# Local attention and two feed-forward layers in one kernel: the order of loads, attention units and weight decoding at the start

## The chip, the cores and the metric

The kernel runs on one core of one Trainium2 chip. The metric is the device time of one execution in microseconds (us). Before the change the median of 3 runs is 875.22 us (874.82 to 875.95).

## The reference

```python
def reference(**kwargs):
    attn_out = _attn_ref(...)                 # 4 batches, 8 heads, 512 local + 32 global rows, head size 64
    x = attn_out.transpose(0, 2, 1, 3).reshape(B * S, H * D)      # 2176 x 512
    x = _moe_ref(x=x, ...)                    # h = x @ w_in; g = elu(h); g @ w_out   (512 -> 2048 -> 512)
    return _moe2_ref(x=x, ...)                # rms norm; silu(xn @ w_gate) * (xn @ w_val) @ w_out
```

Local queries see the local keys within 32 positions and the 32 global keys; each row goes through a softmax. All weights arrive as 64-bit floats.

## The kernel before

**The pieces.** The attention of the local rows is cut into 16 units of 128 queries and all 8 heads (four units are one block of 512 rows). A unit has five pieces. `a_S` (L227) makes the scores: 8 mask matmuls with the `identr` matrix (L237) and 32 products of keys and queries from the tile `kq` (L243), into two tiles `s`. `a_E` (L247) takes the row maxima on the VectorE (DVE, L262 and L263) and the exponentials on the ScalarE (ACT, L265). `a_T` (L268) transposes the exponentials on the TensorE (PE, L271) and ACT copies them out (L273). `a_PV` (L276) multiplies them with the values of the tile `v` (L284). `a_N` (L288) divides by the row sums on DVE (L297 to L299) and writes the unit's part of `x`. When four units are done, `a_X` (L301) transposes the block on PE (L307), ACT rounds it to a high part (L308), and DVE takes what the rounding left, the low part (L309).

**The first expert layer.** `moe_block` (L339) then runs 16 steps over a block. Step j makes h with 12 matmuls (`mm1`, L132), the activation (ACT L121 and L122, DVE L123), its high and low part `g` (ACT L139, DVE L140), and one step later the second product with 12 matmuls (`mm2`, L153). The next block's attention units stand between these steps, a unit in every four of them.

**The weights.** `w_in` and `w_out` come as 16 raw tiles of 1 MB (512 x 512 doubles in two row groups), in the order of `order1`: two tiles of `w_in` and two of `w_out` for each group of four steps. A tile is decoded to a high and a low single-precision part in four operations: `w1_abs` on ACT (L85), `w1_bits` on DVE (L92, L93), `w1_hi` on ACT (L96), `w1_lo` on DVE (L99). Tiles 0 and 1 feed the first four steps of `mm1`, tiles 2 and 3 the first four of `mm2`. Raw tiles 0, 2, 4, ... share two buffers, so raw tile 4 may be loaded only after `w1_bits(0)`, and raw tile 6 only after `w1_bits(2)`.

**What sets the order.** All loads are issued by the SyncE (SP) in one queue. Eight of them can be under way: the ninth waits until the first has landed, and so on. PE runs in the order in which the program is written. In the stretch that the change touches, DVE and ACT do so too (`manual_schedule`, L419):

```python
        with tc.manual_schedule(engines={mybir.EngineType.DVE, mybir.EngineType.Activation}):
            nc.scalar.copy(identr, ident)
            ...
            w1_abs(0)
            a_S(0, ATT2)
            w1_bits(0)
            a_E(0)
            a_S(1, HB)
```

After that stretch, and for SP throughout, a scheduler that works when the kernel is built sets the order. Each engine executes in its order: an instruction that waits holds up all that stand behind it on that engine. The first four units take their keys and values in buffers of the weight pool (`load_kq` L208, `load_v` L217), so none of these loads waits for an earlier one to be used up. `a_X(0, (2, 3), ...)` puts its transposes into the two `h` buffers, so the first `mm1` must wait until DVE has read the third of the four.

**Later stages.** Block 0 decodes the tiles 3 to 15 between its steps; the blocks 1 and 2 prepare the second layer's weights; then come the global attention rows and the second expert layer, which begins after some 440 us and is bound by PE.

Of the kernel before, what the change touches and what calls it, by code (L numbers as in the profile page):

```python
# [40 lines left out]
def fused_kernel(ctx: ExitStack, tc: tile.TileContext, kq, vl, gkq, gv, w_in, w_out, w_gate, w_val, w_o2, rms_g, consts, out):  # L41
# [66 lines left out]
    def new_xT():  # L108
        return [moe.tile([P, 2, 512], F32R, tag=f"xT{c}", name=f"xT{c}") for c in range(4)]
# [84 lines left out]
    with ExitStack() as ls:  # L194
# [13 lines left out]
        def load_kq(u):  # L208
            if u < 16:
                if u < 4:  # L210
                    t = wpool.tile([P, 4, KC], F32, tag="w", name="kq0")
                else:
                    t = ap_.tile([P, 4, KC], F32, tag="kq", name="kq_")
                nc.sync.dma_start(out=t, in_=kq[u].rearrange("p (a n) -> p a n", a=4))
                kq_t[u] = t

        def load_v(u):  # L217
            if u < 16:
                if u < 4:
                    t = wpool.tile([P, 2112], F32, tag="w", name="v0")  # L220
                else:
                    t = ap_.tile([P, 2112], F32, tag="v", name="v_")
                t = t[:, :2080].rearrange("p (i h d) -> p i h d", i=4, h=8)
                nc.sync.dma_start(out=t, in_=vl[u].rearrange("p (i h d) -> p i h d", i=4, h=8))
                v_t[u] = t
# [50 lines left out]
        def a_PV(u, pools):  # L276
            e_t.pop(u)
            b, T = u // 4, u % 4
            ets, v = [et_t.pop((u, par)) for par in range(2)], v_t.pop(u)
            os_ = [pools[i][0].tile([P, 4, 65], F32, tag=pools[i][1], name="o") for i in range(2)]  # L280
            for par in range(2):
                for pr in range(4):
                    for i in range(4):
                        nc.tensor.matmul(os_[par][32 * i:32 * i + 32, pr, :], ets[par][:, pr * P + 32 * i:pr * P + 32 * i + 32], v[:, i, 2 * pr + par, :],  # L284
                                         start=True, stop=True)
            o_t[u] = os_
# [25 lines left out]
        ATT2 = [(aps, "att")] * 4  # L312
# [62 lines left out]
        def w1_load(n=1):  # L375
            for _ in range(n):
                i = n_raw[0]
                if i < 16:
                    wp = i % 2 == 1 and i < 12
                    raws[i] = dec_load(wpool if wp else dec["r"], "w" if wp else "raw", w_src(*order1[i]))  # L380
                    n_raw[0] += 1
# [3 lines left out]
        def w1_abs(i):  # L385
            dxs[i] = dec_abs(dec["t"], raws[i])

        def w1_bits(i):
            dec_bits(dxs[i], raws.pop(i))

        def w1_hi(i):
            kind, a, G = order1[i]
            dst = wpool.tile([P, 2, 2, 512], F32R, tag="w", name="wA")
            for k in range(2):
                if kind == "1":
                    W1[a + k, G] = dst[:, k]
                else:
                    W2[a + k] = dst[:, k]
            split_hi(dst, dxs[i])
            dsts[i] = dst  # L400

        def w1_lo(i):
            split_lo(dsts.pop(i), dxs.pop(i))
            n_dec[0] = i + 1
# [9 lines left out]

        HB = [(hps, "h")] * 2
        Y2 = [(yps, "y2"), (yps, "y3")]
        w1_load()
        load_v(0)
        with tc.manual_schedule(engines={mybir.EngineType.DVE, mybir.EngineType.Activation}):  # L419
            nc.scalar.copy(identr, ident)  # L420
            nc.scalar.copy(masks, mk)
            load_kq(1)
            load_v(1)
            w1_load()
            load_kq(2)
            load_v(2)
            load_kq(3)
            load_v(3)
            w1_load(3)
            w1_abs(0)  # L430
            a_S(0, ATT2)
            w1_bits(0)
            a_E(0)
            a_S(1, HB)
            a_T(0, 0, yps, "y0")
            a_T(0, 1, yps, "y1")
            w1_hi(0)
            a_E(1)
            a_PV(0, Y2)
            w1_lo(0)  # L440
            a_N(0)
            w1_abs(1)
            a_S(2, ATT2)
            a_T(1, 0, yps, "y0")
            a_T(1, 1, yps, "y1")
            a_E(2)
            w1_bits(1)
            a_PV(1, Y2)
            a_N(1)
            a_S(3, HB)  # L450
            a_T(2, 0, yps, "y0")
            a_T(2, 1, yps, "y1")
            a_E(3)
            w1_hi(1)
            a_PV(2, Y2)
            a_N(2)
            a_T(3, 0, yps, "y0")
            a_T(3, 1, yps, "y1")
            w1_lo(1)
            w1_abs(2)  # L460
            a_PV(3, Y2)
            a_N(3)
            xT_t = {0: new_xT()}
            a_X(0, (0, 1), xT_t[0], ATT2[:2] + HB)
            last = a_X(0, (2, 3), xT_t[0], ATT2[:2] + HB)
            w1_bits(2)
            w1_hi(2)
            w1_lo(2)
# [570 lines left out]
    for k in range(2):  # L1039
# [96 lines left out]
        for n in range(7):  # L1136
# [5 lines left out]
            last = n in (3, 5, 6)  # L1142
# [175 lines left out]
```

## Time and profile before

| | |
|---|---|
| median of 3 runs | 875.22 us |
| profiled execution, its own time | 874.71 us |
| its span, first to last instruction | 872.9 us |
| PE busy in matmuls | 847.9 us (97%) |
| DVE busy | 570.8 us (65%) |
| ACT busy | 461.8 us (53%) |
| moved by DMA | 165.69 MB, mean 190 GB/s |
| first `mm1` of block 0 begins | 39.65 us |

A profile shows one execution. "Busy" is the time in which an engine has an instruction at work. An instruction's row has its start, its length and, in brackets, how long the engine had been idle and which engine's work released it. "issue" as a releaser means that the profile shows nothing that the engine waited for. PEclk is the clock that TensorE was granted, as a share of its full 2.4 GHz; 0.5 is its lower level of 1.2 GHz. All times below count from the start of the span.

### The profile page before, as it was taken

The page shows a single profiled execution, that of the slowest core. Times are in us where ns is not written, and L with a number is a line of the kernel's source. Part 1 is how long each engine was busy: PE and PEld are TensorE (multiplying, and loading weights), DVE is VectorE, ACT ScalarE, POOL GpSimd, SP SyncE. Part 2 cuts the span into 40 slices and gives each one's busy share as a digit, 9 for nine tenths or more (in the row PEclk, how much of TensorE's full clock was granted, in tenths as well). Part 3 has the DMA queues.
Part 4 walks back from the last instruction along what each step waited for, and adds up shares of the span by engine and source line. Part 5 has one row for each costly group of instructions (what it writes and reads, how often), then busy time and mean ns, then how long its engine had stood idle before and what let it go on. Part 6 is the DMA issues. An engine that isn't in the chain of part 4 may idle for free.

```text
span 872.9 us, 16265 instructions
## 1 busy us (share of the span) xinstructions
PE 847.9 (97%) x6706; PEld 709.8 (81%) x6706; DVE 570.8 (65%) x1022; ACT 461.8 (53%) x790; POOL 8.0 (1%) x10
## 2 busy tenths in 40 slices
PE   4889999999999999999999999999999999999998
PEld 3667888888888888777878888878999888888998
DVE  3799737656575565544468787897987655555663
ACT  4688645555564455433264677764555444443442
POOL 0000000000000000000030000000000000000000
PEclk9899999999999999999999999999999999999999
DMA  9795625765687665442510687779623232329102
GB/s 361 314 376 191 258 84 188 263 240 200 222 280 285 220 230 210 168 165 97 161 36 25 213 294 242 251 249 330 264 73 120 73 97 74 97 65 404 62 25 86
DMA packets 92271, 165.69 MB, mean 190 GB/s; under 512 B 4900, under 2 KB 59428, under 8 KB 87076
## 3 DMA queue, kind: packets, MB, share of 16 engines
q1 hardware_dynamic: 92196, 164.65, 53.9%
q8 instruction: 53, 0.87, 0.4%
q14 instruction: 22, 0.18, 0.1%
HBM read 128.45 MB, written 36.18 MB: 189 GB/s over the span
## 4 chain that ended last, share of the span: by engine, by line
PE 90%; DMA 3%; ACT 3%; DVE 2%; issue 1%; POOL 0%; DVEq 0%; ACTq 0%
PE y L153 19%; PE h L132 19%; PE A L814 14%; PE c L1163 14%; PE Q L814 11%; DMA kq<-in_kq 2%; PE pg L828 2%; PE o L284 2%; PE s L243 2%; PE ptp L271 2%; PE yg L744 1%; PE og L848 1%; DMA ya<-yT 1%; PE go L966 1%; PE xtp L307 1%
## 5 line engine op out<-in xcount | busy, mean ns | idle before, releaser
L153 PE MATMUL y<-g,wA 128*128 128x512 f32 x768 | 195.8, 398 | 3.7 <-DVE g L140 2.5
L132 PE MATMUL h<-xT,wA 128*128 128x512 f32 x768 | 186.6, 392 | 1.3 <-DVE xT L309 1.3
L153 PEld LDWEIGHTS y<-g,wA 128*128 128x128 f32 x768 | 139.6, 188 | 38.4 <-issue 5.3
L132 PEld LDWEIGHTS h<-xT,wA 128*128 128x128 f32 x768 | 143.6, 188 | 32.1 <-DVE xT L309 1.5
L814 PE MATMUL A<-xc,wS 128*128 128x512 f32 x576 | 138.9, 392 | 0.1
L814 PEld LDWEIGHTS A<-xc,wS 128*128 128x128 f32 x576 | 107.0, 188 | 23.2 <-DVE pp L867 0.8
L1163 PE MATMUL c<-wH,p 128*128 128x256 f32 x1008 | 125.3, 283 | 0.0
L1163 PEld LDWEIGHTS c<-wH,p 128*128 128x128 f32 x1008 | 123.0, 192 | 0.2
L814 PE MATMUL Q<-xc,wS 128*128 128x512 f32 x432 | 104.4, 390 | 0.7 <-DVE t L858 0.7
L814 PEld LDWEIGHTS Q<-xc,wS 128*128 128x128 f32 x432 | 80.2, 188 | 17.5 <-DVE t L858 1.2
L858 DVE TENSOR_TENSOR t<-t,Q 128x512 f32<-128x512 f32 x72 | 48.9, 684 | 48.9 <-ACT t L861 33.7
L853 ACT CAST p<-pp 128x512 fp32r<-128x512 f32 x84 | 51.3, 620 | 55.7 <-PE c L1163 50.8
L121 ACT ACTIVATE e<-h 128x512 f32<-128x512 f32 x48 | 28.8, 600 | 95.9 <-PE h L132 95.9
L861 ACT COPY t<-A 128x512 f32<-128x512 f32 x72 | 42.0, 586 | 62.2 <-PE A L814 62.1
L854 DVE TENSOR_TENSOR p<-pp,p 128x512 fp32r<-128x512 f32 x84 | 56.7, 686 | 21.6 <-ACT p L853 21.6
L123 DVE SCALAR_TENSOR_TENSOR e<-e,h 128x512 f32<-128x512 f32 x48 | 32.8, 683 | 55.1 <-ACT e L122 54.8
L619 DVE TENSOR_TENSOR wS<-wraw,wS 128x1024 fp32r<-128x1024 f32 x42 | 51.2, 1218 | 15.2 <-ACT wS L618 15.1
L139 ACT CAST g<-e 128x512 fp32r<-128x512 f32 x64 | 39.8, 621 | 34.7 <-DVE e L123 21.3
L140 DVE TENSOR_TENSOR g<-e,g 128x512 fp32r<-128x512 f32 x64 | 44.0, 688 | 19.3 <-ACT g L139 18.8
L618 ACT CAST wS<-wraw 128x1024 fp32r<-128x1024 f32 x42 | 43.9, 1045 | 2.0 <-DMA wraw<-wS 2.0
L864 ACT ACTIVATE t<-t 128x512 f32<-128x512 f32 x36 | 22.8, 632 | 39.0 <-DVE t L858 39.0
L93 DVE SCALAR_TENSOR_TENSOR dx<-raw,dx 128x1024 int32<-128x1024 int32 x34 | 41.6, 1229 | 0.9
(201 smaller groups left out, 892.9 us busy)
## 6 DMA issues: line engine op xcount, KB each, us to landing
wH<-wH SPq DMA_DIRECT2D x20, 1024.0 KB, 8.7
wraw<-wS SPq DMA_DIRECT2D x36, 512.0 KB, 4.2
raw<-in_moe_w_out SPq DMA_DIRECT2D x14, 1024.0 KB, 6.6
raw<-in_moe_w_in SPq DMA_DIRECT2D x8, 1024.0 KB, 7.0
raw<-in_moe_w_gate SPq DMA_DIRECT2D x6, 1024.0 KB, 5.9
raw<-in_moe_w_val SPq DMA_DIRECT2D x6, 1024.0 KB, 5.8
wS<-raw SPq DMA_DIRECT2D x24, 256.0 KB, 2.3
gvr<-in_gv SPq DMA_DIRECT2D x8, 640.0 KB, 4.2
```

The source lines that it names most:

```text
L93: nc.vector.scalar_tensor_tensor(out=i32(x), in0=word[:, :, 0], scalar=29, in1=i32(x), op0=ALU.logical_shift_right, op1=ALU.bitwise_or)
L132: nc.tensor.matmul(h[:, :n], W1[c, G][:, ws, o:o + P], xT[c][:, xs, :n], start=(k == 0), stop=(k == 11))
L140: mark[:] = hi, nc.vector.tensor_tensor(out=g[:, 1, :n], in0=e[:, :n], in1=f(g[:, 0, :n]), op=ALU.subtract)
L153: nc.tensor.matmul(ys[dc][:, :n], W2[j][:, ws, dc * P:(dc + 1) * P], g[:, gs, :n], start=(j == 0 and k == 0), stop=(j == 15 and k == 2))
L618: nc.scalar.copy(t[:, :, 0, :], raw)
L619: nc.vector.tensor_tensor(out=t[:, :, 1, :], in0=raw, in1=f(t[:, :, 0, :]), op=ALU.subtract)
L814: nc.tensor.matmul(ps, w[:, 2 * (q % 4) + c, ws, :], x[:, c, xs, :], start=(first and c == 0 and z == 0), stop=(c == 1 and z == 2), skip_g ...
L853: hi = nc.scalar.copy(p[:, 0, :], src)
L854: mark[:] = hi, nc.vector.tensor_tensor(out=p[:, 1, :], in0=src, in1=f(p[:, 0, :]), op=ALU.subtract)
L858: mark[1] = nc.vector.tensor_tensor(out=t, in0=t, in1=ps, op=ALU.add)
L861: mark[0] = nc.scalar.copy(t, ps)
L1163: nc.tensor.matmul(ch[t // 2][:, 256 * (t % 2):256 * (t % 2) + 256], p[:, pl, t * P:(t + 1) * P], w[:, wl, :], start=(n in (0, 1, 3) and i ...
```

## The change

Before, the loads of raw weight tiles and of the units' keys and values alternate, and the decoding of tiles 0, 1 and the first operation of tile 2 is laid between the pieces of the units. The change issues the keys and values of the units 0 to 3 first (raw tile 0 ahead of the last values, raw tiles 1 to 3 behind them). It moves all decoding behind `a_PV(2)`: tile 0 goes between the last pieces of the units 2 and 3, tile 1 begins between the two halves of `a_X` and is finished after it, together with tile 2. On PE, `a_S(2)` moves ahead of `a_PV(0)`, and `a_S(3)` ahead of `a_PV(1)`. No instruction is added or dropped, and no size is changed.

```diff
--- before.py
+++ after.py
@@ -414,55 +414,54 @@
 
         HB = [(hps, "h")] * 2
         Y2 = [(yps, "y2"), (yps, "y3")]
+        load_kq(1)
+        load_v(0)
+        load_kq(2)
+        load_v(1)
+        load_kq(3)
+        load_v(2)
         w1_load()
-        load_v(0)
+        load_v(3)
+        w1_load(3)
         with tc.manual_schedule(engines={mybir.EngineType.DVE, mybir.EngineType.Activation}):
             nc.scalar.copy(identr, ident)
             nc.scalar.copy(masks, mk)
-            load_kq(1)
-            load_v(1)
-            w1_load()
-            load_kq(2)
-            load_v(2)
-            load_kq(3)
-            load_v(3)
-            w1_load(3)
-            w1_abs(0)
             a_S(0, ATT2)
-            w1_bits(0)
             a_E(0)
             a_S(1, HB)
             a_T(0, 0, yps, "y0")
             a_T(0, 1, yps, "y1")
-            w1_hi(0)
             a_E(1)
+            a_S(2, ATT2)
             a_PV(0, Y2)
-            w1_lo(0)
             a_N(0)
-            w1_abs(1)
-            a_S(2, ATT2)
             a_T(1, 0, yps, "y0")
             a_T(1, 1, yps, "y1")
             a_E(2)
-            w1_bits(1)
+            a_S(3, HB)
             a_PV(1, Y2)
             a_N(1)
-            a_S(3, HB)
             a_T(2, 0, yps, "y0")
             a_T(2, 1, yps, "y1")
             a_E(3)
-            w1_hi(1)
             a_PV(2, Y2)
+            w1_abs(0)
             a_N(2)
             a_T(3, 0, yps, "y0")
             a_T(3, 1, yps, "y1")
+            w1_bits(0)
+            a_PV(3, Y2)
+            w1_hi(0)
+            a_N(3)
+            xT_t = {0: new_xT()}
+            w1_lo(0)
+            a_X(0, (0, 1), xT_t[0], ATT2[:2] + HB)
+            w1_abs(1)
+            last = a_X(0, (2, 3), xT_t[0], ATT2[:2] + HB)
+            w1_bits(1)
+            w1_hi(1)
             w1_lo(1)
             w1_abs(2)
-            a_PV(3, Y2)
-            a_N(3)
-            xT_t = {0: new_xT()}
-            a_X(0, (0, 1), xT_t[0], ATT2[:2] + HB)
-            last = a_X(0, (2, 3), xT_t[0], ATT2[:2] + HB)
             w1_bits(2)
             w1_hi(2)
             w1_lo(2)
```

**SP, the first loads.** `kq` and `v` are the units' keys with queries and values (0.72 and 1.06 MB each), `raw` with `w_in` or `w_out` a raw weight tile (1.05 MB). The three rows ahead of these, the first unit's `kq` and two tables, are the same in both. Before:

```order
L74 DMA raw<-in_moe_w_in 128x2x512
L224 DMA v_112<-in_vl 128x2080
L214 DMA kq_118<-in_kq 128x1408
L224 DMA v_120<-in_vl 128x2080
L74 DMA raw<-in_moe_w_in 128x2x512
L214 DMA kq_124<-in_kq 128x1408
L224 DMA v_126<-in_vl 128x2080
L214 DMA kq_128<-in_kq 128x1408
L224 DMA v_130<-in_vl 128x2080
L74 DMA raw<-in_moe_w_out 128x2x512 x2
```

Now:

```order
L214 DMA kq_110<-in_kq 128x1408
L224 DMA v_112<-in_vl 128x2080
L214 DMA kq_114<-in_kq 128x1408
L224 DMA v_116<-in_vl 128x2080
L214 DMA kq_118<-in_kq 128x1408
L224 DMA v_120<-in_vl 128x2080
L74 DMA raw<-in_moe_w_in 128x2x512
L224 DMA v_124<-in_vl 128x2080
L74 DMA raw<-in_moe_w_in 128x2x512
L74 DMA raw<-in_moe_w_out 128x2x512 x2
```

The units' tiles come before the weight tiles, and the keys of unit 1 are the fourth load. Further on, where the scheduler sets SP's order, raw tile 7 stands behind raw tile 8, which waits for `w1_bits(4)`, and raw tile 9 behind raw tile 10, which waits for `w1_bits(6)`; before, the tiles 7 and 9 stood ahead of these waits.

**DVE, from the end of `a_X` to the low part of the first `g`.** `dx`, `raw` and `wA` belong to the decoding of a weight tile, `mx` to unit 4, `e` and `g` to step 0. Before:

```order
L309 TENSOR_TENSOR xT_606<-xtp,xT_606 128x512
L92 TENSOR_SCALAR dx<-dx 128x1024 x2
L93 SCALAR_TENSOR_TENSOR dx<-raw,dx 128x1024 x2
L99 TENSOR_TENSOR wA<-dx,wA 128x2x512
L123 SCALAR_TENSOR_TENSOR e<-e,h 128x512
L262 TENSOR_REDUCE mx<-s 128x4 x2
L99 TENSOR_TENSOR wA<-dx,wA 128x2x512
L92 TENSOR_SCALAR dx<-dx 128x1024
L263 TENSOR_SCALAR mx<-mx 128x4
L140 TENSOR_TENSOR g<-e,g 128x512
```

Now:

```order
L309 TENSOR_TENSOR xT_594<-xtp,xT_594 128x512
L92 TENSOR_SCALAR dx<-dx 128x1024
L93 SCALAR_TENSOR_TENSOR dx<-raw,dx 128x1024
L99 TENSOR_TENSOR wA<-dx,wA 128x2x512
L92 TENSOR_SCALAR dx<-dx 128x1024
L93 SCALAR_TENSOR_TENSOR dx<-raw,dx 128x1024
L92 TENSOR_SCALAR dx<-dx 128x1024
L123 SCALAR_TENSOR_TENSOR e<-e,h 128x512
L93 SCALAR_TENSOR_TENSOR dx<-raw,dx 128x1024
L99 TENSOR_TENSOR wA<-dx,wA 128x2x512
L262 TENSOR_REDUCE mx<-s 128x4 x2
L140 TENSOR_TENSOR g<-e,g 128x512
```

Before, the tiles 2 and 3 are decoded here, and the first operation on tile 4 (L92). Now tile 1 stands first (L92, L93, L99), then tile 2, and the last operation of tile 3 and the first of tile 4 come behind `g`.

**DVE, up to the low part of the third `g`** (step 2; the rows with `st` and `x` normalise unit 4). Before:

```order
L92 TENSOR_SCALAR dx<-dx 128x1024
L298 RECIPROCAL st<-st 128x4
L123 SCALAR_TENSOR_TENSOR e<-e,h 128x512
L298 RECIPROCAL st<-st 128x4
L93 SCALAR_TENSOR_TENSOR dx<-raw,dx 128x1024
L299 TENSOR_TENSOR x<-o,st 128x4x64
L99 TENSOR_TENSOR wA<-dx,wA 128x2x512
L299 TENSOR_TENSOR x<-o,st 128x4x64
L140 TENSOR_TENSOR g<-e,g 128x512
L99 TENSOR_TENSOR wA<-dx,wA 128x2x512
L92 TENSOR_SCALAR dx<-dx 128x1024
```

Now:

```order
L92 TENSOR_SCALAR dx<-dx 128x1024
L299 TENSOR_TENSOR x<-o,st 128x4x64
L297 TENSOR_SCALAR st<-o 128x4
L93 SCALAR_TENSOR_TENSOR dx<-raw,dx 128x1024
L298 RECIPROCAL st<-st 128x4
L99 TENSOR_TENSOR wA<-dx,wA 128x2x512
L123 SCALAR_TENSOR_TENSOR e<-e,h 128x512
L299 TENSOR_TENSOR x<-o,st 128x4x64
L99 TENSOR_TENSOR wA<-dx,wA 128x2x512
L92 TENSOR_SCALAR dx<-dx 128x1024
L140 TENSOR_TENSOR g<-e,g 128x512
```

Before, the low part of the third `g` stands ahead of the last operation on tile 7 (L99) and the first on tile 8 (L92). Now it stands behind both.

## Rows read from the trace of the kernel before

**Rows 1.** The page, part 1: busy time of each engine, share, instructions.

```profile
PE 847.9 (97%) x6706; PEld 709.8 (81%) x6706; DVE 570.8 (65%) x1022; ACT 461.8 (53%) x790; POOL 8.0 (1%) x10
```

**Rows 2.** Chain of waits, first 60 us: start, length, what held it.

```profile
5.03 15.76 DMA kq<-in_kq
...
29.19 2.24 issue
```

**Rows 3.** Timeline, PE, units' stretch: start, length, engine, line, operation, [idle before <-releaser].

```profile
9.20 0.62 PE L237 MATMUL s<-masks,identr 128*32 128x256 bf16 x8
13.32 1.96 PE L243 MATMUL s<-kq 64*32 64x128 f32 x64 [3.50 <-DMA kq<-in_kq]
...
19.35 0.29 PE L237 MATMUL s<-masks,identr 128*32 128x256 bf16 x2 [0.63 <-issue]
...
31.43 1.09 PE L284 MATMUL o<-v,ET 128*32 128x65 f32 x30 [2.24 <-issue]
```

**Rows 4.** Windows, three stretches: PE, PEld, DVE, ACT, POOL busy (xcount), PEclk, DMA share, GB/s.

```profile
13.55:19.34 5.79, 5.17 (x142) 4.01 (x127) 2.46 (x7) 4.51 (x13) 0.00 (x0) 1.00 1.02 420
19.34:25.43 6.09, 4.86 (x125) 3.90 (x128) 4.46 (x13) 4.00 (x11) 0.00 (x0) 0.72 1.02 424
25.43:31.42 5.99, 3.52 (x142) 2.71 (x132) 4.60 (x14) 5.38 (x18) 0.00 (x0) 0.96 1.02 415
```

**Rows 5.** The page, part 3: the instruction queue: packets, MB, share.

```profile
q8 instruction: 53, 0.87, 0.4%
```

**Rows 6.** DMA queues, 28.9 to 31.5 us: the instruction queue's packets, MB, share.

```profile
q8 instruction: 1, 0.02, 2.2%
```

**Rows 7.** Windows, while block 0 runs (columns as in rows 4).

```profile
60.00:70.00 10.00, 10.00 (x66) 7.65 (x72) 10.00 (x15) 7.43 (x10) 0.00 (x0) 1.00 0.90 335
78.00:85.00 7.00, 6.15 (x91) 4.99 (x89) 5.75 (x7) 6.72 (x10) 0.00 (x0) 1.00 0.48 152
```

**Rows 8.** Timeline, PE, second products of the steps 0, 2 and 5.

```profile
49.75 1.42 PE L153 MATMUL y<-g,wA 128*128 128x512 f32 x5 [1.95 <-DVE g L140]
...
63.72 3.07 PE L153 MATMUL y<-g,wA 128*128 128x512 f32 x12
...
84.80 0.50 PE L153 MATMUL y<-g,wA 128*128 128x512 f32 x1 [0.85 <-ACT g L139]
85.86 2.77 PE L153 MATMUL y<-g,wA 128*128 128x512 f32 x11 [0.56 <-DVE g L140]
```

**Rows 9.** Timeline, ACT, the front.

```profile
9.15 1.12 ACT L85 ACTIVATE dx<-raw 128x1024 f32<-128x1024 f32 x1 [2.44 <-DMA raw<-in_moe_w_in]
13.17 2.18 ACT L265 ACTIVATE E<-s,mx 128x128 f32<-128x128 f32 x8 [2.89 <-DVE mx L263]
```

**Rows 10.** Timeline, SP's DMA issues.

```profile
23.31 0.38 SPq L473 DMA_DIRECT2D cst<-in_moe_rms_g  x1
...
42.60 0.37 SPq L74 DMA_DIRECT2D raw<-in_moe_w_out  x1
```

**Rows 11.** Timeline, all engines, around the first `mm1`.

```profile
37.71 2.48 DVE L309 TENSOR_TENSOR xT<-xtp,xT 128x512 fp32r<-128x512 f32 x4 [1.04 <-ACT xT L308]
...
39.65 3.02 PE L132 MATMUL h<-xT,wA 128*128 128x512 f32 x12 [1.28 <-DVE xT L309]
...
44.27 1.23 DVE L99 TENSOR_TENSOR wA<-dx,wA 128x1024 fp32r<-128x1024 f32 x1 [0.60 <-ACT wA L96]
```

**Rows 12.** Groups by line, 40 to 93 us, DVE then ACT: xcount, busy, mean ns, idle before.

```profile
L93 DVE SCALAR_TENSOR_TENSOR dx<-raw,dx 128x1024 int32<-128x1024 int32 x13 | 15.8, 1227 | 0.1
L99 DVE TENSOR_TENSOR wA<-dx,wA 128x1024 fp32r<-128x1024 f32 x12 | 14.6, 1216 | 2.0 <-ACT wA L96 2.0
L92 DVE TENSOR_SCALAR dx<-dx 128x1024 int32<-128x1024 int32 x13 | 8.7, 681 | 0.7 <-ACT dx L85 0.7
...
L85 ACT ACTIVATE dx<-raw 128x1024 f32<-128x1024 f32 x12 | 14.0, 1179 | 1.5 <-DVE g L140 0.8 <-DVE wA L99 0.4 <-DMA raw<-in_moe_w_in 0.3
L96 ACT CAST wA<-dx 128x1024 fp32r<-128x1024 f32 x12 | 12.8, 1066 | 1.5 <-DVE dx L93 1.5
```

## The prediction

> **What bounds the kernel now.** The page first: PE is busy for 97% of the span [rows 1]. So a change at the front is worth what it moves the start of PE's uninterrupted work, and no more. The chain of waits over the first 60 us has two long links that are not PE's: a load of keys (15.76 us) and 2.24 us that the profile can't name [rows 2]. The timeline of PE shows where they are felt: unit 1's scores wait 3.50 us for their keys and begin at 13.32, and PE stands still twice with nothing to wait for, 0.63 us before 19.35 and 2.24 us before 31.43, the second time in the middle of unit 2's value product [rows 3].
>
> The windows tell more of these two gaps. Between 13.55 and 31.42 PE executes 269, 253 and 274 instructions (matmuls and weight loads) in 5.79, 6.09 and 5.99 us, and DMA is full all the while, share 1.02 [rows 4]. The gaps lie at the ends of the first and the third stretch. The instruction queue moved 0.87 MB in 53 packets, 16.4 KB each, for PE's 6706 + 6706 instructions: 253 a packet [rows 1, 5]. One such packet falls beside the long gap [rows 6]. I read it so: PE's instructions come in blocks of about 256, the next block is asked for when one is used up, and it takes 6 us while bulk loads fill the queues. The attention units, with their many small matmuls, then go at 256 instructions in 6 us, however early their data is.
>
> The Trainium skill ("Runtime: NRT & Kernel Launch", section Instruction fetch mechanics) gives the block as 16 KiB or 256 instructions, which the packets here agree with. It calls the cost of crossing into the next block mostly hidden; the gap of 2.24 us doesn't look hidden. By that rule the time would be that of rival A below.
>
> Once block 0 runs, DVE is the other limit. From 60 to 70 us both PE and DVE are busy for 10.00 of 10.00 us; from 78 to 85 DVE for 5.75 of 7.00 [rows 7]. PE waits for DVE's or ACT's part of `g` at step 0 (1.95 us, until 49.75) and at step 5 (0.85 and 0.56 us), and starts step 2's second product at 63.72 without a wait [rows 8].
>
> **The change, part by part.** Durations are those of the profiled execution: 872.9 us span and 1.8 us around it, 874.71 us, which is 0.51 under the median.
>
> *The units start earlier.* The fourth load of before, a raw tile of 1.05 MB, has landed at 9.15 [rows 9]. The fourth is now unit 1's `kq` with 0.72 MB, so it is there when the mask matmuls of unit 1 end, at 9.20 + 0.62 = 9.8 [rows 3]. Unit 1's scores move from 13.32 to 9.8, 3.5 us earlier. The same PE work stands ahead of unit 2's value product as before, in another order, so the gap in its middle comes at the same instruction. If the three blocks take 5.79 + 6.09 + 5.99 = 17.87 us again [rows 4], it ends at 31.43 - 3.5 = 27.9. The bounds are far apart: no gain at all, if the first block does not come earlier, and some 4.4 us more, if blocks hold nothing (rivals C and A). I take 3.5, since the rows show all three blocks at one pace.
>
> *The raw tiles land later.* In the order of bytes, unit 2's values ended at 7.72 MB. They were in by 23.31, when SP, with eight loads under way at most, could issue the eighth after them [rows 10]. Raw tile 0 now ends at 7.39 MB, so it is in by then. At 420 GB/s [rows 4] raw tile 1 (9.50 MB) is in by 27.6, tile 2 by 30.1 and tile 3 by 32.6. ACT turns to tile 0 only behind unit 3's exponentials, about when unit 2's product is resumed (27.9), and to tile 1 only behind two casts of `a_X`, some 7 us later. So this costs nothing; the units' pieces cover it, and with units 5 us faster tile 0 and then tile 1 would be late next. Raw tile 6 waits, as before, for `w1_bits(2)`; its load goes from 42.60 [rows 10] to about 44, ahead of its need.
>
> *Tile 0 on the units' way.* `w1_bits(0)` (1.9 us on DVE) falls where DVE waits for unit 3's value product: nothing, at most 1.9 if that product were ready. `w1_lo(0)`, 1.22 us [rows 12], stands on DVE between unit 3's part of `x` and the first low part of `xT`; `w1_abs(1)`, 1.18 us on ACT, between the second and the third cast. They run side by side, so I count 1.2 once (bounds 0 and 2.4). Before, from the restart at 31.43 to the end of the low parts, 37.71 + 2.48 = 40.19 [rows 11], it took 8.76 us. Now the low parts end at 27.9 + 8.76 + 1.2 = 37.9, 2.3 us ahead.
>
> *Tile 1 behind `a_X`.* It was hidden under the units' waits and is now in the open: L92, L93, L99 are 0.68 + 1.23 + 1.22 = 3.1 us of DVE, which also waits 1.07 us in between for ACT's cast (L96) [rows 12]: 4.2 us. The first `mm1` can do its first half at about 37.5, but the other half needs tile 1, done at 37.9 + 4.2 = 42.1; with four matmuls of 3.02/12 us left it ends at 43.1, where it ended at 39.65 + 3.02 = 42.7 before [rows 11]. The 2.3 us are gone already.
>
> *DVE up to the first `g`.* Before, 9.5 us from 40.19 to 49.7. Now 4.2 more for tile 1, and less what moved behind `g`: 1.22 (tile 3), 0.68 (tile 4), and a wait of 0.60 for tile 2's cast [rows 11], which is now covered. 37.9 + 9.5 + 4.2 - 2.5 = 49.1, 0.6 ahead.
>
> *DVE up to the third `g`.* Before, 14.2 us from 49.7 to 63.9, which is just when PE needs it [rows 8]. Now the 1.9 us of tiles 3 and 4 come in here, and the last operation of tile 7 and the first of tile 8 (1.22 + 0.68) have moved ahead of this `g`. DVE is full in this stretch [rows 7], so all of it counts: 49.1 + 14.2 + 1.9 + 1.9 = 67.1. PE starts that product 3.2 us later than before.
>
> *What is given back.* From here DVE as a whole is behind by 4.2 - 2.3 = 1.9 us. At step 5 PE lost 0.85 + 0.56 = 1.41 us to DVE and ACT [rows 8]; coming 3.2 us later it does not lose them again. What stays is the larger of 1.9 (DVE) and 3.2 - 1.41 = 1.8 (PE): 1.9. The raw tiles 7 and 9 now stand behind waits on SP. That costs nothing if they still land in time and at most one transfer, 2.5 us (1.05 MB at 420 GB/s), if not; I take 0.4, since DVE reaches tile 7 only shortly after it would land.
>
> **The sum** is 1.9 + 0.4 = 2.3 us: 877.0 us against the 874.71 of the profiled execution, 877.5 against the median of 875.22. The case's own range is 876.0 to 879.3. What a measurement can tell from no change is 0.2%, or 1.75 us.
>
> **The rivals.** *A, faster: blocks of instructions hold nothing.* Then the two gaps had another cause and the units go at the pace of ACT and DVE. The exponentials take 2.18 us [rows 9], the copies and the steps between the engines about as much again: an estimate of 4.5 us a unit, not 6. Over three units that is 4.4 us: the restart comes at 23.5, the low parts end at 33.5, DVE is 6.7 - 4.2 = 2.5 us ahead. PE's third `g` is ready 1.2 us early and the 1.41 us of step 5 go: about -2.5, 872.7 us. The change wins from the point where the low parts end 4.2 us earlier than before, that is, where unit 2's value product is resumed before 26.0. For it: the chain names the keys for 15.76 us [rows 2], and that is what the change moves. Against it: 2.24 us of standstill amid one unit's product, whose values had landed six us before [rows 10].
>
> *B, no change: DVE makes good what it lost.* It is idle for 1.25 us between 78 and 85 [rows 7]. If its order costs PE less at the third `g` than I count, only 1.9 - 1.25 = 0.7 us stay: 875.9. Against it: it is idle there because ACT and a load are late, and these are late with it.
>
> *C, slower by more: the first block of instructions comes no earlier.* It needs to wait for the bulk loads ahead of it, which are as many as before. Then PE resumes at 31.43 as it did, all of the decoding is on top, and 3.5 more is lost: 881.0.
>
> **How the numbers follow.** The forecast has a chance of 0.40, A 0.25, B 0.25, C 0.10. Two thirds of the forecast, and C, are slower by over 0.2%; with a little of B that is 0.38. A is faster by over 0.2% in most of its range: 0.20 with the luck of the other terms. The rest, 0.42, is within 0.2%. The range runs from A's time, 872.7, to 880.4, near C's; about half of A and half of C fall outside.
>
> **What would show it.** The profile of the changed kernel should have unit 1's scores at about 9.8 without a wait for keys; a gap without a named cause amid unit 2's value product, ending near 28; the last low part of `xT` near 38; the first `mm1` torn in two, its end near 43; PE's wait for step 0's `g` until about 49, and one for step 2's `g` until about 67; and less than 1.4 us of waits at step 5. The forecast is wrong if that value product is resumed before 26 (A) or after 30 (C), or if step 2's product starts before 65 (B).

## The result and the profile after

The changed kernel takes 880.99 us (median of 4 runs, 880.33 to 881.9) against 875.02 of the kernel before in the same job (874.52 to 875.95): ratio 1.007, 95% interval 1.0057 to 1.0083. It is slower by 6.0 us. The forecast was 877.5, and the range ended at 880.4.

The page: PE is busy for 3.0 us more with the same 6706 matmuls [rows 1], and the first layer's first products (L132) wait 4.5 us in all, before 1.3.

```profile
PE 850.9 (97%) x6706; PEld 710.3 (81%) x6706; DVE 571.5 (65%) x1022; ACT 461.8 (52%) x790; POOL 8.0 (1%) x10
...
L153 PE MATMUL y<-g,wA 128*128 128x512 f32 x768 | 198.8, 402 | 4.1 <-DVE g L140 3.0
L132 PE MATMUL h<-xT,wA 128*128 128x512 f32 x768 | 187.7, 393 | 4.5 <-DVE xT L309 2.1
```

The timeline of PE, from unit 1's scores to step 2's product (start, length, engine, line, operation, count, idle before and what released it):

```profile
9.76 1.28 PE L243 MATMUL s<-kq 64*32 64x128 f32 x64
...
21.26 0.62 PE L243 MATMUL s<-kq 64*32 64x128 f32 x19 [2.46 <-issue]
...
28.24 1.09 PE L284 MATMUL o<-v,ET 128*32 128x65 f32 x30 [3.24 <-issue]
...
37.80 1.66 PE L132 MATMUL h<-xT,wA 128*128 128x512 f32 x6 [2.09 <-DVE xT L309]
41.34 0.73 PE L132 MATMUL h<-xT,wA 128*128 128x512 f32 x2 [1.88 <-ACT wA L96]
42.60 1.20 PE L132 MATMUL h<-xT,wA 128*128 128x512 f32 x4 [0.53 <-DVE wA L99]
...
49.95 1.42 PE L153 MATMUL y<-g,wA 128*128 128x512 f32 x5 [1.56 <-DVE g L140]
52.33 0.66 PE L271 MATMUL ptp<-ident,E 128*128 128x128 f32 x4 [0.97 <-ACT E L265]
54.76 1.12 PE L271 MATMUL ptp<-ident,E 128*128 128x128 f32 x4 [1.77 <-ACT E L265]
55.53 2.70 PE L153 MATMUL y<-g,wA 128*128 128x512 f32 x6
...
68.67 0.50 PE L153 MATMUL y<-g,wA 128*128 128x512 f32 x1 [0.98 <-ACT g L139]
70.27 4.02 PE L153 MATMUL y<-g,wA 128*128 128x512 f32 x11 [1.10 <-DVE g L140]
74.09 3.29 PE L132 MATMUL h<-xT,wA 128*128 128x512 f32 x12
```

Up to the first `mm1` this is the forecast: the keys no longer wait, the standstill moved, the first product begins 1.84 us earlier and is torn (into 6, 2 and 4 matmuls). Then two things show. PE waits at more places than before. And matmuls take longer: eleven of step 2 need 4.02 us, where twelve needed 3.07 [rows 8]. The windows say why (PE, PEld, DVE, ACT and POOL busy, PEclk, DMA share, GB/s):

```profile
51.00:54.40 3.40, 1.02 (x6) 0.42 (x4) 3.18 (x7) 3.00 (x9) 0.00 (x0) 1.00 0.60 249
54.44:57.85 3.41, 3.09 (x10) 2.61 (x11) 3.00 (x3) 3.41 (x7) 0.00 (x0) 0.50 0.92 285
67.50:71.40 3.90, 1.82 (x7) 1.15 (x7) 3.90 (x7) 3.23 (x6) 0.00 (x0) 1.00 0.77 325
71.50:74.92 3.42, 3.42 (x9) 2.64 (x8) 3.42 (x5) 2.67 (x4) 0.00 (x0) 0.50 0.66 180
```

The second and the fourth row are the two stretches behind the first `mm1` in which the granted clock was 1.2 GHz; just ahead of them PE had been busy for 1.02 of 3.40 and for 1.82 of 3.90 us. Before, it was 2.4 GHz from 34.4 us on, through a wait of 1.95 us too [rows 8].

The account from the first `mm1` of block 0 to the thirteenth (which begins at 126.75, before at 119.45):

| | before | after | difference |
|---|---|---|---|
| first `mm1` begins | 39.65 | 37.80 | -1.84 |
| waits of PE over 0.1 us, summed | 4.45 | 9.25 | +4.80 |
| the rest, PE at work | 75.36 | 79.70 | +4.34 |
| thirteenth `mm1` begins | 119.45 | 126.75 | +7.30 |

From there the distance stays (7.1 us at the last matmul). The instructions in between are the same. Some 3.4 of the +4.34 us are matmuls at half clock: the two stretches last 6.83 us together, and six matmuls of step 0's product take 2.70 us there, before 1.64. Some 0.6 us went with the first `mm1`, which starts three times, and 0.4 with step 6's product, where twelve matmuls at 98.03 take 3.32 us instead of 2.88.

Who is late? ACT splits unit 4's exponentials by tile 5's first operation, and later stands for 3.25 us, because raw tile 7 isn't there. SP asked for it at 53.98, behind raw tile 8, which had waited for tile 4's decoding. Timeline of ACT, then of SP:

```profile
52.54 1.15 ACT L85 ACTIVATE dx<-raw 128x1024 f32<-128x1024 f32 x1 [0.26 <-DMA raw<-in_moe_w_in]
53.58 1.13 ACT L265 ACTIVATE E<-s,mx 128x128 f32<-128x128 f32 x4
...
62.38 1.12 ACT L85 ACTIVATE dx<-raw 128x1024 f32<-128x1024 f32 x1 [3.25 <-DMA raw<-in_moe_w_out]
```

```profile
53.56 0.37 SPq L74 DMA_DIRECT2D raw<-in_moe_w_in  x1
53.98 7.66 SPq L74 DMA_DIRECT2D raw<-in_moe_w_out  x2
```

And DVE: the first `e` is done at 45.82, and ACT's cast of it at 46.56, yet the low part of `g`, for which PE stands, runs at 49.21. In between DVE decodes tiles 3 and 2 and takes unit 4's maxima; tile 2 is due for this product, tile 3 only for step 2's.

```profile
45.13 0.69 DVE L123 SCALAR_TENSOR_TENSOR e<-e,h 128x512 f32<-128x512 f32 x1
45.74 1.22 DVE L93 SCALAR_TENSOR_TENSOR dx<-raw,dx 128x1024 int32<-128x1024 int32 x1
46.88 1.22 DVE L99 TENSOR_TENSOR wA<-dx,wA 128x1024 fp32r<-128x1024 f32 x1
48.01 1.28 DVE L262 TENSOR_REDUCE mx<-s 128x4 f32<-128x512 f32 x2
49.21 0.68 DVE L140 TENSOR_TENSOR g<-e,g 128x512 fp32r<-128x512 f32 x1
```

So there were four suspects: the place of the decoding and of the loads at the front, the late tile 7, the clock, and the order that the scheduler gives DVE and ACT behind the front. The thirteen runs below take them up in turn. A time with a range is a median; the kernel before took 874.69 to 875.25 us beside them.

### The profile page after: what moved, and what is told of

Its sections match the earlier page's. It is cut to its first block, busy times and chain, and to the rows that moved or that the text cites. A ratio compares the mean times of both kernels' runs of the same rounds, so it can differ in the third digit from the quotient of the medians.

```text
span 880.0 us, 16257 instructions
## 1 busy us (share of the span) xinstructions
PE 850.9 (97%) x6706; PEld 710.3 (81%) x6706; DVE 571.5 (65%) x1022; ACT 461.8 (52%) x790; POOL 8.0 (1%) x10
## 4 chain that ended last, share of the span: by engine, by line
PE 91%; DVE 3%; DMA 2%; ACT 2%; issue 1%; SPq 0%; DVEq 0%; ACTq 0%
PE y L153 20%; PE h L132 18%; PE A L813 14%; PE c L1162 14%; PE Q L813 11%; PE s L243 2%; PE o L284 2%; PE pg L827 2%; PE ptp L271 2%; PE yg L743 1%; PE hg L727 1%; PE og L847 1%; DMA raw<-in_moe_w_out 1%; DMA raw<-in_moe_w_in 1%; PE go L965 1%
## 5 line engine op out<-in xcount | busy, mean ns | idle before, releaser
L153 PE MATMUL y<-g,wA 128*128 128x512 f32 x768 | 198.8, 402 | 4.1 <-DVE g L140 3.0
L132 PE MATMUL h<-xT,wA 128*128 128x512 f32 x768 | 187.7, 393 | 4.5 <-DVE xT L309 2.1
L132 PEld LDWEIGHTS h<-xT,wA 128*128 128x128 f32 x768 | 143.9, 189 | 36.5 <-DVE xT L309 2.3
L153 PEld LDWEIGHTS y<-g,wA 128*128 128x128 f32 x768 | 141.0, 190 | 40.0 <-issue 5.1
L121 ACT ACTIVATE e<-h 128x512 f32<-128x512 f32 x48 | 28.9, 601 | 92.8 <-PE h L132 92.7
L93 DVE SCALAR_TENSOR_TENSOR dx<-raw,dx 128x1024 int32<-128x1024 int32 x34 | 41.6, 1223 | 0.8
```

Source lines behind the costliest of these rows:

```text
L93: nc.vector.scalar_tensor_tensor(out=i32(x), in0=word[:, :, 0], scalar=29, in1=i32(x), op0=ALU.logical_shift_right, op1=ALU.bitwise_or)
L132: nc.tensor.matmul(h[:, :n], W1[c, G][:, ws, o:o + P], xT[c][:, xs, :n], start=(k == 0), stop=(k == 11))
L153: nc.tensor.matmul(ys[dc][:, :n], W2[j][:, ws, dc * P:(dc + 1) * P], g[:, gs, :n], start=(j == 0 and k == 0), stop=(j == 15 and k == 2))
```

## The experiments

### What the standstills at the front are

**nomask**: the changed kernel without the mask matmuls of units 0 to 3, so that PE has 8 matmuls and 8 weight loads less in each unit. The scores of these units stay without their mask.

```diff
-            for s in ss if u < 8 else ():
+            for s in ss if 4 <= u < 8 else ():
...
```

> The changed kernel without the mask matmuls of the units 0 to 3 (8 matmuls and 8 weight loads a unit are left out, so these units see unmasked scores). Block theory (PE's instructions come in blocks of 256, each some 6 us after the one before while DMA is full): the standstills come at the same count of instructions, so 16 instructions later in the program for each unit passed: the one after 45 matmuls of unit 3's scores moves into unit 1's value product, the one after 34 matmuls of unit 2's value product moves into unit 3's transposes, the first one into unit 0's value product. Rival (they wait for data or a buffer): they stay where they are, in unit 3's scores and unit 2's value product.

One run, 879.6 us. Two of the three standstills are still there, and at other instructions:

```profile
21.79 0.99 PE L284 MATMUL o<-v,ET 128*32 128x65 f32 x52 [1.59 <-issue]
...
27.91 1.72 PE L271 MATMUL ptp<-ident,E 128*128 128x128 f32 x7 [2.32 <-ACT E L265]
```

The first now falls 12 matmuls into unit 1's value product (in the changed kernel amid unit 3's scores), the second behind unit 3's first transpose (there amid unit 2's product). The profile puts the second down to ACT. The places go with the number of instructions that PE has behind it, not with data: by the trace's records these two lie behind 697 and 947 matmuls and weight loads, the changed kernel's three behind 447, 699 and 949. The counterpart of the one behind 447 is not seen here; PE waits 1.73 us for unit 2's keys shortly before. The Trainium skill ("Runtime: NRT & Kernel Launch", Instruction fetch mechanics) calls the price of crossing into the next block of 256 "mostly hidden". Here, with the loads running, the same crossings cost 2.46 and 3.24 us in the changed kernel, and the measurement decides.

**held**: the raw tiles 0 to 3 are asked for only once DVE has reached unit 3's maxima (a `memset` of one column of the buffer holds the load back; all raw loads are kept in program order), so that less traffic lies beside the instruction fetch.

```diff
...
+        if hold:
+            nc.vector.memset(raw.rearrange("p a n -> p (a n)").bitcast(F32)[:, 0:1], 0.0)
...
             a_E(3)
+            w1_load(4)
...
```

> The changed kernel with all raw weight tiles held back until unit 3's exponentials have been issued (a one-column write by DVE that the loads must wait for), so that DMA carries only keys and values at first and is quiet from about 20 us. Block theory: the first two standstills stay, and the third, amid unit 2's value product (3.24 us), shrinks below 1.5 us, since its block is fetched while DMA is quiet; that product is resumed before 26.5. Rival (the standstill does not hang on DMA traffic): still near 28. The whole run is slower in either case, by 5 to 12 us, since decoding starts late.

One run, 880.25 us. The standstills were 0.66, 2.46 and 2.69 us, so the third did not shrink below 1.5 us, and the product was resumed at 27.65. That traffic makes the blocks slow isn't borne out, and not refuted either, since the keys and values alone kept DMA full up to 24 us; only then did it ease:

```profile
20.00:24.00 4.00, 2.70 (x91) 2.17 (x90) 1.35 (x6) 1.30 (x5) 0.00 (x0) 1.00 0.99 415
24.00:28.00 4.00, 1.14 (x50) 0.97 (x53) 2.31 (x12) 2.78 (x10) 0.00 (x0) 0.86 0.81 240
```

### Loads or pieces

**oldloads**: the loads in the order of before, the pieces in that of the change.

```diff
-        load_kq(1)
-        load_v(0)
-        load_kq(2)
-        load_v(1)
-        load_kq(3)
-        load_v(2)
-        w1_load()
-        load_v(3)
-        w1_load(3)
+        w1_load()
+        load_v(0)
+        load_kq(1)
+        load_v(1)
+        w1_load()
+        load_kq(2)
+        load_v(2)
+        load_kq(3)
+        load_v(3)
+        w1_load(3)
```

> The changed order of the pieces, but the loads in the order of before (raw tiles 0 and 1 among the keys and values, seven raw tiles ahead of block 0). Theory 1 (it is the moved decoding that costs, and the earlier keys give some 3 us back): unit 1's scores at 13.3, the restart amid unit 2's value product at about 31.4, the last low part of xT at about 41.5; with raw tile 7 in time the run is at 881 to 883. Rival (it is the new order of the loads that costs): back at 875 to 876.

882.72 us (881.54 to 884.78), ratio 1.0089 (1.0071 to 1.0107). Unit 1's scores wait for their keys again (3.84 us, until 13.67), the first `mm1` begins at 42.81, the decoding in the open is on top: what the change loses does not come from the order of its first loads.

**ahead**: the changed kernel asks for six raw tiles ahead of block 0, the kernel before for seven. One more:

```diff
-        w1_load(2)
+        w1_load(3)
```

> The changed kernel with one raw weight tile more loaded ahead of block 0 (7 instead of 6, as before the change). Theory 1 (the change lost time in two ways: the decoding of tiles 0 and 1 moved into the stretch where DVE is full, and raw tile 7, now issued behind raw tile 8, lands late): ACT does not stand still for raw tile 7 (3.2 us in the changed kernel), the third step's second product starts its eleven matmuls near 67.8 us instead of 70.27, and the run is 2 to 4 us faster than the changed kernel, 877 to 879. Theory 2 (the late tile is hidden by DVE's other work): no difference, 880.5 to 881.5.

884.97 us (880.79 to 887.16), ratio 1.0112 (1.0073 to 1.015): a miss. Step 2's product no longer waits, but unit 5's transposes now wait 1.97 and 0.37 us for their exponentials, and the six matmuls behind them take 2.91 us, at half clock. In the profiled execution the whole front was also 2.1 us later, as the mask table landed late, which no part of the edit explains. The wait had moved, not gone.

### The late tile 7

**late7**: the kernel before, with raw tile 7 behind raw tile 8 on SP, as in the changed kernel.

```diff
...
-                if i < 16:
+                n_raw[0] += 1
+                for i in {7: (), 8: (8, 7)}.get(i, (i,)):
...
```

> The kernel before, with raw tile 7 asked for behind raw tile 8 (both kept in that order on SP), as it stands in the changed kernel; the front is as it was. The scheduler then also moves some pieces of DVE and ACT, from the weights of step 2 on. Theory 1 (the late tile 7 costs several us by itself): raw 8 is asked for at about 51 us, once DVE has done with tile 4, raw 7 behind it; ACT stands idle for 1.5 us or more before tile 7, step 2's product waits, the granted clock falls after it, and the time is 876.5 to 879.5. Theory 2 (it costs only where DVE is already behind by the change): 874.2 to 875.8.

878.57 us (877.24 to 880.04), ratio 1.0045 (1.0033 to 1.0057): 3.7 us. ACT's own wait for the tile was only 0.67 us, since other work stood before it. The profiled execution has 3.85 us of delay at the thirteenth `mm1` (123.30, before 119.45). Of these, 0.9 stand ahead of the first `mm1` (40.55, before 39.65), and 0.7 come with half clock that begins at 51.33, before SP asks for tile 7 at 52.28. Behind that 0.65 are lost at step 2's product, and PE waits at unit 5:

```profile
83.07 0.65 PE L273 MATMUL ptp<-ident,E 128*128 128x128 f32 x4 [1.88 <-ACT E L267]
```

So theory 1's time holds, its place only in part; what of it is tile 7's, and what the share of the pieces that the scheduler moved, this run does not tell.

**only78**: the changed kernel with raw tiles 7 and 8 alone kept in program order.

```diff
...
+        if keep:
+            tc.keep_in_program_order(ins)
...
+                    raws[i] = dec_load(wpool if wp else dec["r"], "w" if wp else "raw", w_src(*order1[i]), keep=i in (7, 8))
```

> The changed kernel with only raw tiles 7 and 8 kept in program order on SP. DVE's and ACT's order is then the changed kernel's up to unit 4's part of x, so the halves of unit 4's exponentials stay apart and the first mm1 stays torn. Theory 1 (the late tile 7 is most of what the sum lacked): step 2's product waits under 0.5 us, no half clock near 70, 876.3 to 878. Theory 2 (what helped was the new order of all pieces that came with the order of all loads): 879 to 881.5.

881.06 us (880.13 to 882.0), ratio 1.0072 (1.0051 to 1.0093): no gain. (The edits move line numbers: L155 is L153 here.) Step 2's product starts at 67.49 without a wait, as theory 1 says. But half clock now lasts longer at step 0 (51.98 to 58.80, in the changed kernel 54.44 to 57.85), and the next wait stands at unit 5:

```profile
54.64 2.91 PE L155 MATMUL y<-g,wA 128*128 128x512 f32 x6
57.35 3.60 PE L134 MATMUL h<-xT,wA 128*128 128x512 f32 x12
...
67.49 2.88 PE L155 MATMUL y<-g,wA 128*128 128x512 f32 x12
...
84.21 0.66 PE L273 MATMUL ptp<-ident,E 128*128 128x128 f32 x4 [1.87 <-ACT E L267]
```

**pinned**: all raw loads from tile 5 on in program order (`i >= 5` in the same edit).

> The changed kernel with its raw loads from tile 5 on kept in program order on SP, so that tile 7 is no longer asked for behind a load that waits. All else is as changed. Theory 1 (the late tile 7 is a cause of its own): ACT no longer idles for 3.25 us at 59 to 62, step 2's product waits 0 to 0.5 us instead of 2.08, no half clock follows it, and the time falls by 2.5 to 3.5 us, to 877.5 to 878.5. Theory 2 (the third g is late by the order of DVE's pieces alone): tile 7 lands earlier, the wait stays over 1.5 us, time 880.3 to 881.9.

876.45 us (875.06 to 877.27, 10 runs), ratio 1.002 (1.001 to 1.0029), faster than either theory said. It looks like theory 1, yet "all else is as changed" was not so: the scheduler also gave DVE and ACT another order (unit 4's eight exponentials now stand together, behind tile 5's first operation), and with tiles 7 and 8 alone nothing is gained. What helped came with the rest, the order of the pieces or that of the later loads; this run doesn't tell which.

### The clock

**fill**: 34 matmuls by a tile of zeros in the waits, which add nothing to the sums.

```diff
+    def fill(o, x, n, start=False):
+        for _ in range(n):
+            nc.tensor.matmul(o, zero, x, start=start, stop=False)
...
```

> The changed kernel with 34 extra matmuls by a zero weight tile, laid into four of the waits of PE in block 0 (before the 7th and 9th matmul of the first mm1, before the second matmul of step 0's product, before either half of unit 4's transposes, and before the first and second matmul of step 2's product); they add zero. Theory 1 (the clock: between the first and the thirteenth mm1 the changed kernel lost 4.8 us to waits and 4.3 us to matmuls at half clock, and the waits bring the clock down): the granted clock stays at 1.0 from 45 to 90 us, step 2's product takes 3.0 us instead of 4.0, and the time falls by 1.7 to 3.4 us, to 877.6 to 879.3. Theory 2 (the clock is a by-product, DVE sets the pace): the clock may stay up, but the waits for g grow by what the matmuls save, and the time stays at 880.3 to 881.9.

880.54 us (878.37 to 882.91), ratio 1.0069 (1.0043 to 1.0094). From 41.2 us on the clock stays up:

```profile
54.00:58.00 4.00, 4.00 (x21) 3.38 (x21) 3.42 (x4) 4.00 (x6) 0.00 (x0) 1.00 0.94 314
66.00:71.00 5.00, 5.00 (x24) 4.10 (x23) 4.96 (x7) 4.63 (x6) 0.00 (x0) 1.00 0.64 261
```

The time does not follow. Between the first and the thirteenth `mm1` PE's own matmuls take some 75.6 us, as before the change (75.36), but by their starts in the trace the zeros take 9.6 us, and the waits that are left 3.11, together 3.4 us more than the 9.25 us of waits in the changed kernel. Most of these 3.4 us are a new wait of 2.30 us at step 6, for a `g` whose cast ended at 93.85 and whose low part DVE runs at 95.96, behind two pieces of decoding (PE, then DVE):

```profile
96.70 2.77 PE L164 MATMUL y<-g,wA 128*128 128x512 f32 x11 [2.30 <-DVE g L148]
```

```profile
93.70 1.21 DVE L101 TENSOR_TENSOR wA<-dx,wA 128x1024 fp32r<-128x1024 f32 x1
94.83 1.22 DVE L95 SCALAR_TENSOR_TENSOR dx<-raw,dx 128x1024 int32<-128x1024 int32 x1
95.96 0.68 DVE L148 TENSOR_TENSOR g<-e,g 128x512 fp32r<-128x512 f32 x1
```

**pinned_fill**: both edits.

> Both edits, the raw loads in program order and the zero matmuls in the waits. Clock theory: no half clock after 36 us, time 876 to 877.5, that is, 1.5 us and more under the one with the order alone. DVE theory: as the one with the order alone, within 0.8 us.

876.48 us (876.13 to 877.64), against 876.45 without the zeros: nothing. But here the zeros overdo it. In the profiled executions they take some 9.7 us of PE, while its waits between the first and the thirteenth `mm1` fall by 5.7 us (6.86 to 1.14) and its own matmuls by 2.9 (77.35 to 74.45). So the run does not show that the clock is worth nothing. **fill** shows that a kernel with its clock up can lose the gain at the next wait; a filling that fits its waits was not tried.

### The order behind the front

**gaps_ahead**: keys ahead, raw tiles 0 and 1 between the values, both decoded while the units stand still.

```diff
...
             a_E(1)
+            w1_abs(0)
             a_S(2, ATT2)
...
             a_E(2)
+            w1_bits(0)
+            w1_hi(0)
+            w1_abs(1)
             a_S(3, HB)
...
             a_E(3)
+            w1_lo(0)
+            w1_bits(1)
+            w1_hi(1)
             a_PV(2, Y2)
             a_N(2)
+            w1_lo(1)
```

> Keys ahead as in the change, but raw tiles 0 and 1 loaded between the units' values, seven raw tiles asked for ahead, and tiles 0 and 1 decoded in the standstills of the units (before unit 2's scores, before unit 3's, before unit 2's value product). Theory 1 (what cost the changed kernel is the decoding in the open; the earlier units themselves are worth 2 to 3.5 us): unit 2's value product resumed near 28, last low part of xT near 37, first mm1 whole and by 37, no half clock after 40, time 871.5 to 873.5. Theory 2 (the units cannot be had earlier once two raw tiles lie between their loads, or the front is worth nothing because DVE sets the pace up to 100 us): 874.5 to 876.

874.25 us (871.58 to 875.6), ratio 0.999 (0.9977 to 1.0002). The front does what theory 1 says: last low part of `xT` at 37.9, first `mm1` whole at 37.06. The median lies between the two theories' times, nearer to theory 2's. In the profiled execution, one of the slowest, PE waits 1.59 + 1.78 + 1.14 us around step 0's product, with half clock through most of it:

```profile
46.91:57.15 10.24, 7.73 (x22) 5.97 (x23) 9.70 (x14) 10.24 (x19) 0.00 (x0) 0.50 1.03 421
```

The ten runs differ by 4 us, and their mean granted clock with them: the five at 0.994 and more took 871.58 to 874.31 us, the five at 0.992 and less 874.20 to 875.60. Longer waits and a lower clock come together here, so this does not tell what the clock alone costs.

**gaps_behind**: the same, and every decode in block 0 is issued behind the `g` of its own step.

```diff
-                with tc.issue_after(last[0].ins), tc.issue_after(last[1].ins):
+                with behind(mark):
                     w1_decode()
```

> The kernel with keys ahead, raw tiles 0 and 1 between the units' values and both decoded in the units' standstills, and besides with every later decode in block 0 issued behind the g of its step (behind the mark that act1 leaves) and no longer behind a_X alone. Theory 1 (PE waits in block 0 because DVE decodes tiles that are needed two to four steps later ahead of the g that is needed now): the waits of PE between the first and the thirteenth mm1 fall from 4.5 us to under 2.5, no half clock from 45 us on, time 869.5 to 872.5. Theory 2 (DVE's total is the limit, so that the waits come back at the weights): waits for wA in front of step 2's or 4's products, time 874 to 877.

866.20 us (865.96 to 866.69), ratio 0.9903 (0.9886 to 0.992): faster than the kernel before by 8.7 us and than the changed one by 14.8, and by more than expected. One wait of 0.85 us is left, and the clock stays up (PE, then windows):

```profile
35.78 3.03 PE L132 MATMUL h<-xT,wA 128*128 128x512 f32 x12 [1.29 <-DVE xT L309]
...
45.83 0.66 PE L271 MATMUL ptp<-ident,E 128*128 128x128 f32 x4 [0.85 <-ACT E L265]
```

```profile
31.00:60.00 29.00, 26.16 (x281) 20.81 (x278) 23.19 (x40) 19.66 (x33) 0.00 (x0) 1.00 0.85 330
60.00:110.00 50.00, 50.00 (x476) 40.36 (x476) 37.78 (x60) 35.39 (x59) 0.00 (x0) 1.00 0.50 186
```

From 60 to 110 us PE does not stop, and DVE is busy for 37.8 of 50 us: once its order is right, it is no limit in this stretch.

**after_behind** and **before_behind**: the same one edit on the changed kernel and on the kernel before.

> The changed kernel with one edit, every decode in block 0 from tile 3 on issued behind the g of its step. Raw loads stand where the scheduler puts them, tile 7 no longer behind a wait for tile 4's decode. Theory 1 (it is the order of pieces and loads that made the change lose, not the work in the open): unit 4's halves and step 2's product without waits over 0.5 us, time 871 to 874.5. Theory 2 (tile 1 in the open costs its 4 us whatever follows): 876 to 879.

> The kernel before with one edit, every decode in block 0 from tile 3 on issued behind the g of its step; its front is as it was. The same edit brought the changed kernel from 881.0 to 872.0. Theory 1 (the change costs time in itself, tile 1 in the open and the first mm1 torn): PE's waits between the first and the thirteenth mm1 fall from 4.5 us to about 1, and with the first mm1 at 39.6 the time is 869 to 871. Theory 2 (the earlier units pay for it, the change lost only by the order behind it): 872 to 874.

The changed kernel takes 871.98 us (871.76 to 872.89), ratio 0.9966 (0.9954 to 0.9979), the kernel before 870.59 (870.14 to 870.77), ratio 0.9951 (0.9934 to 0.9968). In the latter DVE goes from `e` over unit 4's maxima to `g` with no decoding between:

```profile
44.59 0.69 DVE L123 SCALAR_TENSOR_TENSOR e<-e,h 128x512 f32<-128x512 f32 x1
45.19 1.28 DVE L262 TENSOR_REDUCE mx<-s 128x4 f32<-128x512 f32 x2
46.39 0.68 DVE L140 TENSOR_TENSOR g<-e,g 128x512 fp32r<-128x512 f32 x1
```

So the decoding in the open is not by itself what made the change lose 6 us. It is still there in after_behind, with the torn `mm1`, and that kernel is 9.0 us below the changed one. Nor is it the order of the loads: against what was expected, SP still asks for tile 7 behind tile 8, at 59.03, but ACT comes to it only at 72.04 and no longer waits for it (after_behind, SP, then ACT):

```profile
58.61 0.37 SPq L74 DMA_DIRECT2D raw<-in_moe_w_in  x1
59.03 0.47 SPq L74 DMA_DIRECT2D raw<-in_moe_w_out  x1
```

```profile
72.04 1.14 ACT L85 ACTIVATE dx<-raw 128x1024 f32<-128x1024 f32 x1
```

With the order mended, the change costs 1.4 us (871.98 - 870.59; the runs of the two don't overlap, their ratios' intervals do). What these are is not settled: in the profiled after_behind half clock lies on the torn `mm1`, where before_behind has none.

```profile
38.48:45.31 6.83, 5.30 (x41) 2.61 (x47) 4.31 (x5) 3.11 (x4) 0.00 (x0) 0.50 0.11 29
```

Nor is the earlier front worth nothing: gaps_behind begins its first `mm1` 4.13 us before before_behind (35.78 and 39.91) and is 4.4 us faster.

## Why the prediction was wrong

| step | forecast | measured |
|---|---|---|
| unit 1's scores begin | 9.8 | 9.76 |
| standstill in unit 2's product ends | 27.9 | 28.24 |
| last low part of `xT` ends | 37.9 | 38.34 |
| first `mm1` ends | 43.1 | 43.8 |
| first `g` ends | 49.1 | 49.89 |
| third `g` ends | 67.1 | 70.21 |
| PE's delay behind it | 3.2 | 7.5 (fifth `mm1`: 74.09, before 66.62) |
| given back at step 5 | 1.41 | 1.1 (7.9 to 6.8) |
| end | +2.3 | +7.2 in the profiled executions |

**Right up to the first `g`.** The reading of the two gaps as blocks of 256 instructions carried the front: all five points there lie within 0.8 us, and **nomask** shows the blocks by themselves. That they agree to some tenths is partly luck: the six kernels with this front (after, after_behind, fill, only78, pinned, pinned_fill) resumed the product between 27.09 and 28.43, each in one execution. Rival A is out (the product was resumed at 28.24, not before 26). Rival C named the time that came, 881.0, but its mechanism did not happen: that restart would have been at 31.43.

**The step that failed is *DVE up to the third `g`***, "67.1 ... PE starts that product 3.2 us later than before", with the 0.4 us for raw tile 7 in *What is given back*. It was a sum of DVE's instructions alone, with every other engine taken as ready and each matmul at full clock. The instructions were counted rightly. The third `g` came 3.1 us late: 0.8 of it were there at the first `g`, and 2.2 came because DVE stood for 2.9 us in between, before for 0.7. The longest of these waits is for ACT's first operation on tile 7 (DVE):

```profile
63.52 0.69 DVE L92 TENSOR_SCALAR dx<-dx 128x1024 int32<-128x1024 int32 x1 [1.50 <-ACT dx L85]
```

The profile of after has three terms that the sum lacks:
- ACT. Tile 5's first operation split unit 4's exponentials, and PE waited 0.97 + 1.77 us where it had waited 0.80.
- Raw tile 7. It was bounded at 2.5 us and taken at 0.4; ACT stood for 3.25 us. The count of loads ahead of block 0, six instead of seven, was in the diff and was overlooked.
- The clock, some 3.4 us.

**But the last two are not the cause by themselves.** With tile 7 late, and what the scheduler moved beside it, the kernel before loses 3.7 us (late7). Yet with tile 7 alone in time the changed kernel takes 881.06, and with the clock held up 880.54: cure one, and PE meets the next late `g` or `E`. The split exponentials were not tried alone, and what the clock alone is worth stays open. What the runs put in place of the step is the order: behind the front DVE and ACT decode tiles that are not needed yet ahead of the `g` and the exponentials for which PE stands. The kernel before got by with 4.45 us of waits; with some 4 us of decoding more in the open they were 9.25. Rival B supposed that DVE's idle 1.25 us would make it good; DVE did have time over (1.20 us between 85.3 and 92.0), but not where PE needed it. The edit that mends the order leaves tile 7 behind tile 8 on SP, so the 9.0 us come with the order of the pieces on DVE and ACT; how they divide among the single waits is not told apart further.

**The size was fair for the work itself.** The forecast's 1.9 us (4.2 for tile 1 in the open, less the 2.3 that the units give) compares with the 1.4 us that the change costs with the order mended. Some luck is in that too, since half clock on the torn `mm1` is no term of the 1.9.

## What to carry to other kernels

When work moves from a gap into a stretch where a helper engine is nearly full, a sum of that engine's instructions is a lower bound: follow each piece that the bottleneck waits for, and look what stands ahead of it in the queue without being due. If such a wait is cured and the time stays, look for the wait that has taken its place before doubting the cure. Here the order behind the change was worth 4.4 us to the kernel before and 9.0 us to the changed one, where the change itself costs 1.4; let producers of what is needed now go first, and prefetching work behind them.

## What the runs showed of the hardware

- While bulk loads ran, PE stood still for 0.94, 2.46 and 3.24 us behind 447, 699 and 949 instructions (matmuls and weight loads) of the changed kernel, with no wait that the profile names. With other instructions in front (**nomask**) it stood behind 697 and 947, at other places of the program.
- The granted clock was 1.2 GHz right behind stretches in which PE had been busy for 1.02 of 3.40 and 1.82 of 3.90 us. The matmuls behind took longer (six of step 0's product 2.70 us, before 1.64), some 3.4 us in all. Matmuls by zeros in the waits kept it at 2.4 GHz from 41.2 us on (**fill**), but took 9.6 us of PE themselves, and the time stayed at 880.54 us.
